# Weight write-back on GpSimd's queue, evacuations first on ScalarE, and weight sums in three spaced parts, in a retention layer with two feed-forward layers

## The chip, the cores and the metric

One core of a Trainium2 chip runs the whole program. The metric is the device time of one execution in microseconds (us), the median of several runs.

The engines are TensorE (PE, matrix products; PEld is its weight load), VectorE (DVE), ScalarE (ACT), GpSimd (POOL) and SyncE (SP). Each works through its own list of instructions in order and waits at the first one whose inputs are not there. A DMA is an instruction on the list of the engine that issues it.

## The reference

```
for t in range(S):                                  # retention, B=2, H=8, S=768, D=64
    state = gamma * state + outer(k[t], v[t])
    y[t] = scale * q[t] @ state
x = y as (1536, 512)
h = x @ w_in1;  g = softplus(h);  x = g @ w_out1     # 512 -> 2048 -> 512
h = x @ w_in2;  g = h * sigmoid(h);  out = g @ w_out2
```

Everything is fp32. The weights reach the chip as 64-bit numbers and are converted there.

## The kernel before, in words

Each fp32 matrix is split into a high part (rounded to the format that TensorE multiplies at full speed) and a low remainder, and one product is three matmuls: low x high, high x low, high x high.

**First layer.** After the retention chunks, 48 steps run: each is one of 16 column blocks `fc` of the first layer for one of three blocks of 512 tokens. `step(i)` issues, in this order, `first(i)` (12 matmuls into a bank `h`, then two softplus passes `act1` on ACT) and `second(i - 2)` (12 matmuls into the accumulators acc0 to acc3). The subtraction `act2(i)` on DVE makes the low part of `g`, which `second(i)` needs two steps later. The last step of a run of 3 to 5 blocks evacuates: acc0 and acc1 are copied out and seeded again on ACT (L512, L516), acc2 and acc3 are added out on DVE (L518). Until acc0 is seeded, the next `second` can't start.

**Conversion jobs.** In the gaps of DVE and ACT runs the conversion of weights, listed by `_jobs`: 64 tiles (16 `fc`, two layers, w_in and w_out) and 8 "forms". A tile is one exponent pass on ACT (L363, `w_exponent`), five or six DVE operations (L370 or L375 and L376, then L384, L387, L390, L392) and one rounding pass on ACT (L405, `w_split`). Tiles are loaded by SP (L335, three buffers; L344, the `near` copy, two buffers; the next load of a buffer is issued when its tile has been read).

**Forms.** The second layer's first product is done in seven half-size products per pair of column blocks (P1 to P7, by sums of quarter blocks as in Strassen's scheme, Winograd's form), so the weights of each pair need four sums. `w_sums` (DVE, L413 to L419) adds the two tiles' parts from `st1` into `w32` and makes the sums; `w_sums_high` (ACT, L422) rounds them; `w_keep` (DVE, L425) makes the remainders and writes everything to DRAM (`d1`, 1.8 MB, L428). The converted w_out tiles go through `st2` and `w32` to DRAM as `d2` (0.5 MB each, L409). There is one `st1` and one `w32`: the next pair's w_in tiles (L392 into `st1`) wait for the landing of `d1`, and the next `w_sums` (L413 into `w32`) waits for the landing of the `d2` write from `w32`. All these writes are issued by SP, in one list with the loads.

**Second layer.** 16 pair steps (two token halves of 8 pairs). A pair step issues the seven products in the order P1, P6, P2, P7, P5, P4, P3, and between them units (three matmuls each, L637) of the pair before. Three PSUM banks rotate over two buffers: `bx`, then `by` as a copy of `bx` (ACT, L677), then `bz`. P6 can't start until the copy is there; the copy needs P1 and a free buffer, which is that of the pair before's `bz`, read last by DVE at L695. `silu(q, c)` is two ACT passes (L619, L620) and one DVE subtraction (L621). Four of them per pair make `g`. The conversion jobs that are left (15) run in `slot()` after P1, P6 and P5.

Of the kernel before, what the change touches and what calls it, by code (L numbers as in the profile page):

```python
# [71 lines left out]
LATE = (43, 44, 45, 46, 47)  # L72


def _jobs(steps):


    first, last = {}, {}
    for i, (_, _, fc, _, _) in enumerate(steps):
        for s in range(2):  # L80
            first.setdefault((fc, s), i + LAG * s)
            last[fc, s] = i + LAG * s
    jobs = [("tile", 0, *u) for u in ((0, 0, -2), (1, 0, -1), (2, 0, 0), (0, 1, 2), (1, 1, 3), (2, 1, 4))]
    jobs += [("tile", 0, *u) for u in ((3, 0, 5), (4, 0, 6), (3, 1, 7))]
    left = sorted(set(first) - {j[2:4] for j in jobs}, key=lambda u: (first[u], u))
    second = []
    for p in range(NPR):
        a, b = 2 * p, 2 * p + 1
        second += [("tile", 1, a, 0), ("tile", 1, b, 0), ("forms", 1, p, 0), ("tile", 1, a, 1), ("tile", 1, b, 1)]
    room = 0.0  # L90
    for at in range(8, len(steps)):
        room = min(room, 3.0) + STEP_ROOM - 0.75
        i = at - LAG
        if steps[i][4]:
            room -= 1.4
        ready = [u for u in left if last.get((u[0] - NSLOT, u[1]), -1) < at]
        n = 0
        if ready and (room >= TILE_COST or first[ready[0]] <= at + 4):
            u = ready[0]
            assert at < first[u] - (u[1] == 0), (u, at, first[u])  # L100
            left.remove(u)
            jobs.append(("tile", 0, *u, at))
            room -= TILE_COST
            n += 1
        urgent = left and first[left[0]] <= at + 5
        if at >= 10 and at not in LATE and not urgent:
            while n < 2 and room >= (cost := FORMS_COST if second[0][0] == "forms" else TILE_COST):
                if second[0][0] == "forms" and jobs[-1][1] == 1 and jobs[-1][4] == at:
                    break
                jobs.append((*second.pop(0), at))  # L110
                room -= cost
                n = 2 if jobs[-1][0] == "forms" else n + 1
    assert not left
    return jobs + [(*j, None) for j in second]
# [17 lines left out]
def retention_ffn2_kernel(  # L132
# [268 lines left out]
    def w_split(u):  # L401
        _, l, fc, s, _ = tiles[u]
        a = conv_t.pop(u)[0]
        hi, lo = w_home(u)
        nc.scalar.activation(out=hi, in_=a, func=AF.Copy)  # L405
        w_t[l, fc, s] = (hi, lo)
        if l == 1 and s == 1:
            o = fc % 2 * 1024
            nc.sync.dma_start(out=d2[fc // 2][:, o : o + 1024], in_=(st2, w32)[fc % 2])  # L409

    def w_sums():

# [11 lines left out]
    def w_keep(p):  # L424
        nc.vector.tensor_tensor(  # L425
            out=st1[:, 3072:4096].bitcast(F32R), in0=st1[:, 3072:4096], in1=st1[:, 1024:2048], op=ALU.subtract
        )
        nc.sync.dma_start(out=_rows(d1[p], 2), in_=_rows(st1, 2)[:, :, QF:2048])  # L428

    h_t, g_t, acc_t = {}, {}, {}  # L430
    part = rp.rearrange("p (m t) -> p m t", m=4)
# [231 lines left out]
    def pair_step(q, fill, work):  # L663
# [10 lines left out]
        for n, (name, _, _) in enumerate(PRODUCTS):  # L674
            if name == "P1":
                product(q, n, new("bx"), True)
                nc.scalar.activation(out=new("by"), in_=bank["bx"], func=AF.Copy)  # L677
            elif name == "P6":
                product(q, n, bank["by"], False)
                nc.scalar.activation(out=c["u2"], in_=bank["by"], func=AF.Copy)  # L680
# [9 lines left out]
            elif name == "P4":  # L690
                product(q, n, bank["by"], False)
                silu(q, (1, 0), bank["by"])
            else:
                product(q, n, bank["bz"], False)
                nc.vector.tensor_tensor(out=c["c12"], in0=bank["bz"], in1=c["u2"], op=ALU.add)  # L695
                q1_load(q + 2)
            for w in work.get(name, ()):
                w()
            if name == "P5":
                silu(q, (1, 1), c["c22"])  # L700
            elif name == "P3":
                silu(q, (0, 1), c["c12"])
            for _ in range(gaps[n]):
                fill.pop(0)()
        q2_load(q + 1)
# [18 lines left out]
    def job_end(j):  # L724
        if j[0] == "tile":
            w_split(order[j[:4]])
        else:
            w_sums_high()

    def job_last(j):  # L730
        if j[0] == "forms":
            w_keep(j[2])

    split_units = []

    def step(i, more=()):
        nonlocal split_units
        first(i)
        ended = split_units
        for j in ended:  # L740
            job_end(j)
        split_units = units.get(i, [])
        for j in split_units:
            job_start(j)
        second(i - LAG)
        for j in split_units:
            job_main(j)
        for j in ended:
            job_last(j)
        act2(i)  # L750
        for w in more:
            w()

# [5 lines left out]
    with tc.manual_schedule():  # L759
# [149 lines left out]

        def slot():  # L910

            ended = before.copy()
            for j in ended:
                job_end(j)
            before.clear()
            if pending:
                j = pending.pop(0)
                if j[0] == "tile" and order[j[:4]] not in conv_t:
# [2 lines left out]
                    job_start(pending[0])  # L921
                job_main(j)
                before.append(j)
            for j in ended:
                job_last(j)

        x1 = []
        for q in range(NQ):
# [13 lines left out]
                    work[name], x1[:k] = tuple(x1[:k]), []  # L942
            pair_step(q, fill, work)
            fill = units_of(q)
        for f in fill:
            f()

# [59 lines left out]
```

## Time and profile before

| | us |
|---|---|
| median of 3 runs (lowest, highest) | 582.14 (579.09, 585.39) |
| the profiled execution: its time | 582.73 |
| its span | 580.6 |
| PE busy | 562.8 (97%) |
| DVE busy | 353.7 (61%) |
| ACT busy | 267.3 (46%) |
| POOL busy, all of it in the first 60 us | 25.6 (4%) |

The span is what the profiler saw; the 2.1 us between it and the time lie around it. PE's busy time is the sum of stretches in which a matmul is under way, so a matmul that runs at half clock counts as busy too. What can be gained without changing the matmuls is PE's idle time and the time lost to a lower granted clock. In the row of the page with 40 slices that clock is full but for slice 16 (0.7) and slice 26 (0.9).

### The profile page before, as it was taken

What the parts mean: (1) busy time and instruction counts of PE and PEld (TensorE: products, weight loads), DVE (VectorE), ACT (ScalarE), POOL (GpSimd) and SP (SyncE); (2) the same over time, 40 slices, a digit from 0 to 9 for tenths busy, and PEclk for the clock granted to TensorE, in tenths of its full rate; (3) what the DMA queues carried; (4) which work ended last, traced back from release to release, by engine and by line L of the source; (5) the groups of instructions that cost most, each with busy time, mean ns of one, the idle gap of its engine ahead of it and who ended that gap; (6) DMA issues with size and microseconds to landing.
All of it is one profiled execution on the core that took longest, in us unless ns stands there. A gap on an engine that the chain in (4) does not pass through costs nothing.

```text
span 580.6 us, 8107 instructions
## 1 busy us (share of the span) xinstructions
PE 562.8 (97%) x3122; PEld 479.9 (83%) x3122; DVE 353.7 (61%) x621; ACT 267.3 (46%) x500; POOL 25.6 (4%) x24
## 2 busy tenths in 40 slices
PE   8999999999989989999999999899999999999997
PEld 5888888888868867888788878788989999999996
DVE  2988837797887868696973896776553322212122
ACT  2355534565563634645654553553453333332322
POOL 1554000000000000000000000000000000000000
PEclk9999999999999997999999999899999999999999
DMA  8993333685997678788675789876920534444522
GB/s 297 399 411 112 109 110 110 216 304 204 358 355 271 238 263 317 277 330 300 225 274 214 294 298 360 335 305 251 339 82 20 195 116 170 165 183 185 200 72 108
DMA packets 30149, 136.04 MB, mean 234 GB/s; under 512 B 3360, under 2 KB 3360, under 8 KB 26272
## 3 DMA queue, kind: packets, MB, share of 16 engines
q1 hardware_dynamic: 30112, 135.54, 63.5%
q8 instruction: 24, 0.39, 0.3%
q14 instruction: 13, 0.11, 0.1%
HBM read 109.32 MB, written 26.21 MB: 233 GB/s over the span
## 4 chain that ended last, share of the span: by engine, by line
PE 71%; DVE 13%; DMA 9%; ACT 4%; issue 1%; SPq 1%; POOL 0%; DVEq 0%; POOLq 0%
PE acc L637 19%; PE acc L495 17%; PE h L455 15%; PE by L605 8%; PE bx L605 5%; PE bz L605 5%; DMA d<-w 4%; DMA near<-in_wts 2%; DVE rc L387 2%; DMA d<-st 1%; DMA rp<-in_att 1%; PE sc L235 1%; PE py L253 1%; DVE rc L384 1%; DVE rc L390 1%
## 5 line engine op out<-in xcount | busy, mean ns | idle before, releaser
L495 PE MATMUL acc<-rg,rw 128*128 128x512 f32 x564 | 140.0, 396 | 5.0 <-ACT acc L516 4.4
L455 PE MATMUL h<-rx,rw 128*128 128x512 f32 (+1 forms) x588 | 139.9, 387 | 0.1
L495 PEld LDWEIGHTS acc<-rg,rw 128*128 128x128 f32 x564 | 106.8, 191 | 29.2 <-ACT acc L516 5.9
L455 PEld LDWEIGHTS h<-rx,rw 128*128 128x128 f32 x588 | 109.0, 189 | 23.0 <-DVE rx L298 0.3
L637 PE MATMUL acc<-rw,rg 128*128 128x512 f32 x477 | 125.4, 392 | 0.0
L637 PEld LDWEIGHTS acc<-rw,rg 128*128 128x128 f32 x477 | 88.7, 188 | 12.3
L621 DVE TENSOR_TENSOR rg<-re,rg 128x384 fp32r<-128x384 f32 x53 | 29.3, 557 | 71.1 <-ACT re L620 71.1
L474 ACT ACTIVATE rg<-h 128x512 fp32r<-128x512 f32 x47 | 28.0, 596 | 92.2 <-PE h L455 92.1
L619 ACT ACTIVATE rg<-rp 128x384 fp32r<-128x384 f32 x32 | 16.8, 525 | 63.7 <-DVE rp L695 32.3
L387 DVE SCALAR_TENSOR_TENSOR rc<-rc 128x512 uint32<-128x512 uint32 x64 | 44.3, 692 | 2.2
L363 ACT ACTIVATE rc<-rc 128x512 f32<-128x512 f32 x64 | 41.5, 665 | 5.7 <-DMA rc<-in_wts 5.4
L384 DVE TENSOR_SCALAR rc<-rc 128x512 uint32<-128x512 uint32 x64 | 27.0, 422 | 16.8 <-ACT rc L363 16.8
L481 DVE TENSOR_TENSOR rg<-re,rg 128x512 fp32r<-128x512 f32 x47 | 34.0, 724 | 3.8 <-ACT re L475 3.7
L605 PE MATMUL by<-rx,rw 128*128 128x384 f32 x144 | 30.4, 347 | 4.8 <-ACT by L677 4.8
L605 PEld LDWEIGHTS by<-rx,rw 128*128 128x128 f32 x144 | 26.2, 192 | 8.2 <-ACT by L677 6.5
L689 DVE TENSOR_TENSOR rp<-bz,rp 128x384 f32<-128x384 f32 x16 | 8.9, 557 | 38.8 <-PE bz L605 38.8
L605 PE MATMUL by<-f,rw 128*128 128x384 f32 x144 | 29.2, 337 | 0.0
L390 DVE TENSOR_SCALAR rc<-rc 128x512 uint32<-128x512 uint32 x64 | 27.3, 427 | 2.2
L475 ACT ACTIVATE re<-h 128x512 f32<-128x512 f32 x48 | 28.5, 593 | 0.0
L605 PEld LDWEIGHTS by<-f,rw 128*128 128x128 f32 x144 | 25.9, 188 | 2.0
L405 ACT ACTIVATE rw<-rc 128x512 fp32r<-128x512 f32 x32 | 20.2, 633 | 15.7 <-DVE rc L387 15.7
L637 PE MATMUL acc<-rw,rx 128*128 128x512 f32 x99 | 27.1, 399 | 0.0
(86 smaller groups left out, 636.2 us busy)
## 6 DMA issues: line engine op xcount, KB each, us to landing
rc<-in_wts SPq DMA_DIRECT2D x64, 512.0 KB, 4.9
rw<-d SPq DMA_DIRECT2D x14, 1792.0 KB, 7.8
near<-in_wts SPq DMA_DIRECT2D x41, 511.5 KB, 4.7
d<-st SPq DMA_DIRECT2D x8, 1792.0 KB, 6.9
rw<-d SPq DMA_DIRECT2D x14, 1024.0 KB, 9.2
rp<-in_att SPq DMA_DIRECT2D x8, 512.0 KB, 7.5
d<-st SPq DMA_DIRECT2D x8, 512.0 KB, 8.6
d<-w SPq DMA_DIRECT2D x8, 512.0 KB, 9.2
```

What stands on the lines that cost most here:

```text
L363: nc.scalar.activation(out=z, in_=raw_t[u][:, :, 1].bitcast(F32), func=AF.Copy, scale=2.0**-112)
L384: nc.vector.tensor_scalar(out=z, in0=z, scalar1=3, scalar2=4, op0=ALU.logical_shift_left, op1=ALU.bitwise_or)
L387: nc.vector.scalar_tensor_tensor(out=a, in0=raw[:, :, 1], scalar=0x80000000, in1=z, op0=ALU.bitwise_and, op1=ALU.bitwise_or)
L390: nc.vector.tensor_scalar(out=z, in0=a, scalar1=0xFF800000, scalar2=None, op0=ALU.bitwise_and)
L455: nc.tensor.matmul(ph[:, t], lhsT=w[:, s], rhs=x[:, kc, t], start=kc == o == j == 0, stop=kc == NPAIR - 1 and j == 2, skip_group_check=i == 0,
L474: nc.scalar.activation(out=ghi, in_=ph, func=AF.Softplus)
L475: nc.scalar.activation(out=t, in_=ph, func=AF.Softplus)
L481: nc.vector.tensor_tensor(out=glo, in0=t, in1=ghi.bitcast(F32), op=ALU.subtract)
L495: nc.tensor.matmul(acc_t[m], lhsT=lhsT, rhs=rhs, start=first and j == 0 and not seeded, stop=last and j == 2, skip_group_check=m in SEEDED,)
L605: nc.tensor.matmul(to, lhsT=a[:, s], rhs=x[:, kc, :], start=start and kc == j == 0, stop=kc == 1 and j == 2, skip_group_check=True,)
L621: nc.vector.tensor_tensor(out=glo, in0=r, in1=ghi.bitcast(F32), op=ALU.subtract)
L637: nc.tensor.matmul(acc2_t[m], lhsT=a[:, s], rhs=b, start=start and j == 0, stop=stop and j == 2)
```

## The change

Five edits:

1. The writes of `d1` and `d2` are issued from GpSimd's list instead of SP's.
2. In a step that evacuates, the exponent passes (`job_start`) are issued behind `second` and its evacuation, not ahead of it.
3. The forms are spread out: `w_sums` in step i, `w_sums_high` at the end of step i + 1 (behind everything else that ACT does there), `w_keep` in step i + 2 behind the evacuation. Before, `w_sums_high` stood in step i + 1 ahead of the evacuation and `w_keep` at the end of the job work of step i + 1. In the second layer the slots are spread in the same way.
4. `not_before` keeps uses of `st1` and `w32` apart: a pair's first tile goes no earlier than three steps behind the forms before it, forms no earlier than two steps behind the last tile in `w32`. Of the list of jobs this moves two: tile (1, 4, 0) from step 27 to 28, where (1, 5, 0) already was, and tile (1, 8, 0) from step 39 to 40, where (1, 9, 0) already was.
5. In a pair step `silu` of P3's result goes behind the next pair's copy (L677 before), and `silu` of P5's result behind that of P4's.

```diff
+def not_before(job, done):
+    what, _, k, s = job
+    if what == "forms":
+        return max(done["tile", 1, 2 * k + 1, 0] + 1, done.get(("tile", 1, 2 * k - 1, 1), -9) + 2)
+    if s == 0:
+        return done.get(("forms", 1, k // 2 - 1, 0), -9) + 3
+    return max(done["forms", 1, k // 2, 0] + 1, done.get(("tile", 1, k - 2, 1), -9) + 2)
...
-                if second[0][0] == "forms" and jobs[-1][1] == 1 and jobs[-1][4] == at:
+                if at < not_before(second[0], done):
                     break
+                done[second[0]] = at
...
-            nc.sync.dma_start(out=d2[fc // 2][:, o : o + 1024], in_=(st2, w32)[fc % 2])
+            nc.gpsimd.dma_start(out=d2[fc // 2][:, o : o + 1024], in_=(st2, w32)[fc % 2])
...
-        nc.sync.dma_start(out=_rows(d1[p], 2), in_=_rows(st1, 2)[:, :, QF:2048])
+        nc.gpsimd.dma_start(out=_rows(d1[p], 2), in_=_rows(st1, 2)[:, :, QF:2048])
...
                 nc.scalar.activation(out=new("by"), in_=bank["bx"], func=AF.Copy)
+                if q:
+                    silu(q - 1, (0, 1), c["c12"])
...
                 silu(q, (1, 0), bank["by"])
+                silu(q, (1, 1), c["c22"])
...
-            if name == "P5":
-                silu(q, (1, 1), c["c22"])
-            elif name == "P3":
-                silu(q, (0, 1), c["c12"])
...
+    def job_after(j):
+        for p in to_split:
+            w_sums_high()
+            to_keep.append(p)
+        to_split.clear()
+        if j and j[0] == "forms":
+            to_split.append(j[2])
+
+    def job_keep():
+        for p in to_keep:
+            w_keep(p)
+        to_keep.clear()
...
         first(i)
-        ended = split_units
-        for j in ended:
+        for j in split_units:
             job_end(j)
         split_units = units.get(i, [])
-        for j in split_units:
-            job_start(j)
+        evacuates = steps[i - LAG][4]
+        if not evacuates:
+            for j in split_units:
+                job_start(j)
         second(i - LAG)
+        if evacuates:
+            for j in split_units:
+                job_start(j)
+        job_keep()
         for j in split_units:
             job_main(j)
-        for j in ended:
-            job_last(j)
         act2(i)
+        job_after(split_units[-1] if split_units else None)
...
-            ended = before.copy()
-            for j in ended:
+            for j in before:
                 job_end(j)
             before.clear()
+            job_keep()
+            done = None
...
-            for j in ended:
-                job_last(j)
+                done = j
+            job_after(done)
```

Line numbers of the changed kernel are higher by 12 to 15 (L422 is L434 there, L512 is L524, L677 is L689). First, ScalarE's list in steps 29 and 30, where the forms of pair 2 meet an evacuation; `st_883` is `st1`, `acc_0` and `acc_1` are the accumulators. Before:

```order
L474 ACTIVATE rg<-h_1868 128x512
L475 ACTIVATE re<-h_1868 128x512
L422 ACTIVATE st_883<-st_883 128x1024
L363 ACTIVATE rc<-rc 128x512 x2
L512 ACTIVATE rp<-acc_0_1724 128x512
L516 ACTIVATE acc_0_1893<-rp 128x512
L512 ACTIVATE rp<-acc_1_1727 128x512
L516 ACTIVATE acc_1_1896<-rp 128x512
```

And after the change:

```order
L486 ACTIVATE rg<-h_1868 128x512
L487 ACTIVATE re<-h_1868 128x512
L524 ACTIVATE rp<-acc_0_1722 128x512
L528 ACTIVATE acc_0_1890<-rp 128x512
L524 ACTIVATE rp<-acc_1_1725 128x512
L528 ACTIVATE acc_1_1893<-rp 128x512
L375 ACTIVATE rc<-rc 128x512 x2
L434 ACTIVATE st_883<-st_883 128x1024
```

The four evacuation passes have moved ahead of the rounding of the sums and of both exponent passes.

Second, ScalarE's list where the second layer's pair 2 ends (`by_2850` is its P4 bank) and pair 3 begins. Before:

```order
L619 ACTIVATE rg<-rp 128x384
L620 ACTIVATE re<-rp 128x384
L619 ACTIVATE rg<-by_2850 128x384
L620 ACTIVATE re<-by_2850 128x384
L619 ACTIVATE rg<-rp 128x384
L620 ACTIVATE re<-rp 128x384
L677 ACTIVATE by_2975<-bx_2968 128x384
L422 ACTIVATE st_883<-st_883 128x1024
L363 ACTIVATE rc<-rc 128x512
```

And after the change:

```order
L631 ACTIVATE rg<-by_2847 128x384
L632 ACTIVATE re<-by_2847 128x384
L631 ACTIVATE rg<-rp 128x384
L632 ACTIVATE re<-rp 128x384
L689 ACTIVATE by_2972<-bx_2965 128x384
L631 ACTIVATE rg<-rp 128x384
L632 ACTIVATE re<-rp 128x384
L375 ACTIVATE rc<-rc 128x512
L434 ACTIVATE st_883<-st_883 128x1024
```

The copy into `by` has moved ahead of the two passes of `silu` on P3's result.

Third, VectorE's list in steps 39 and 40, from the last operation of tile (1, 7, 1) on (`w_884` is `w32`). Before:

```order
L392 SCALAR_TENSOR_TENSOR w_884<-rc 128x512
L425 TENSOR_TENSOR st_883<-st_883 128x1024
L481 TENSOR_TENSOR rg<-re,rg 128x512
L518 TENSOR_TENSOR rp<-acc_2_2107,rp 128x512
L518 TENSOR_TENSOR rp<-acc_3_2111,rp 128x512
L370 TENSOR_SCALAR rc<-near 128x512
L384 TENSOR_SCALAR rc<-rc 128x512
L387 SCALAR_TENSOR_TENSOR rc<-rc 128x512
L390 TENSOR_SCALAR rc<-rc 128x512
L392 SCALAR_TENSOR_TENSOR st_883<-rc 128x512
L481 TENSOR_TENSOR rg<-re,rg 128x512
```

And after the change:

```order
L404 SCALAR_TENSOR_TENSOR w_884<-rc 128x512
L493 TENSOR_TENSOR rg<-re,rg 128x512
L530 TENSOR_TENSOR rp<-acc_2_2107,rp 128x512
L530 TENSOR_TENSOR rp<-acc_3_2111,rp 128x512
L437 TENSOR_TENSOR st_883<-st_883 128x1024
L493 TENSOR_TENSOR rg<-re,rg 128x512
L382 TENSOR_SCALAR rc<-near 128x512
L396 TENSOR_SCALAR rc<-rc 128x512
L399 SCALAR_TENSOR_TENSOR rc<-rc 128x512
L402 TENSOR_SCALAR rc<-rc 128x512
L404 SCALAR_TENSOR_TENSOR st_883<-rc 128x512
```

The remainders (L425, now L437), whose result the 1.8 MB write waits for, have moved behind the evacuation, and between them and the next tile into `st1` there is one subtraction of `act2` where two additions and one subtraction were; the next `act2` now follows two tiles.

## Rows read from the trace of the kernel before

**Rows 1.** Waits of PE from 60 us on: total us, times, longest.

```profile
PE by L605 <- ACT by L677: 4.8, 4, 3.0
PE acc L495 <- ACT acc L516: 4.4, 3, 3.1
PE acc L495 <- DVE rg L481: 0.6, 2, 0.4
PE bz L605 <- ACT re L620: 0.6, 1, 0.6
```

**Rows 2.** Busy time and granted clock (PEclk) of two stretches behind long waits.

```profile
219.00:224.00 5.00, 5.00 (x12) 3.89 (x13) 4.83 (x9) 3.67 (x7) 0.00 (x0) 0.50 0.87 296
364.00:367.00 3.00, 2.09 (x7) 2.09 (x8) 2.42 (x5) 2.42 (x5) 0.00 (x0) 0.68 0.97 410
```

**Rows 3.** The chain that ended last, in order of time: start us, us, what.

```profile
146.49 7.60 DMA near<-in_wts
...
202.10 10.53 DMA d<-w
...
218.94 5.49 PE acc L495 x12
224.43 3.15 PE h L455 x12
227.57 2.72 PE acc L495 x12
...
269.08 6.66 DMA d<-st
...
346.50 12.67 DMA d<-w
...
364.91 2.18 PE by L605 x6
367.09 2.08 PE acc L637 x6
370.23 1.39 PE acc L637 x6
...
379.95 1.06 PE bx L605 x6
```

**Rows 4.** ACT's instructions in order of time, at two long waits of PE.

```profile
215.60 1.06 ACT L422 ACTIVATE st<-st 128x1024 fp32r<-128x1024 f32 x1 [4.08 <-DVE st L419]
216.56 1.21 ACT L363 ACTIVATE rc<-rc 128x512 f32<-128x512 f32 x2
...
363.55 0.52 ACT L619 ACTIVATE rg<-rp 128x384 fp32r<-128x384 f32 x1 [5.59 <-DVE rp L695]
...
364.39 0.47 ACT L677 ACTIVATE by<-bx 128x384 f32<-128x384 f32 x1
```

**Rows 5.** DMA issues of the page: KB each, median us from issue to landing.

```profile
near<-in_wts SPq DMA_DIRECT2D x41, 511.5 KB, 4.7
d<-st SPq DMA_DIRECT2D x8, 1792.0 KB, 6.9
```

**Rows 6.** DVE's instructions in order of time, around two writes from `st1`.

```profile
194.76 1.22 DVE L425 TENSOR_TENSOR st<-st 128x1024 fp32r<-128x1024 f32 x1
...
267.84 1.22 DVE L425 TENSOR_TENSOR st<-st 128x1024 fp32r<-128x1024 f32 x1
...
275.83 0.69 DVE L392 SCALAR_TENSOR_TENSOR st<-rc 128x512 fp32r<-128x512 int32 x1 [3.12 <-DMA d<-st]
...
277.04 0.42 DVE L370 TENSOR_SCALAR rc<-near 128x512 uint32<-128x512 uint32 x1
...
279.64 0.68 DVE L481 TENSOR_TENSOR rg<-re,rg 128x512 fp32r<-128x512 f32 x1
```

**Rows 7.** PE's matmuls of `second` in steps 30 and 42.

```profile
210.24 2.88 PE L495 MATMUL acc<-rg,rw 128*128 128x512 f32 x12
...
282.53 2.88 PE L495 MATMUL acc<-rg,rw 128*128 128x512 f32 x12
```

More of the change, by code (lines that the diff above doesn't have):

```diff
@@ L89, in _jobs @@
         second += [("tile", 1, a, 0), ("tile", 1, b, 0), ("forms", 1, p, 0), ("tile", 1, a, 1), ("tile", 1, b, 1)]
+    done = {}
     room = 0.0
@@ L726, in job_end @@
             w_split(order[j[:4]])
-        else:
+    to_split, to_keep = [], []
+    def job_after(j):
+        for p in to_split:
             w_sums_high()
-    def job_last(j):
-        if j[0] == "forms":
-            w_keep(j[2])
+            to_keep.append(p)
[6 more added lines that the diff above has]
+        to_keep.clear()
     split_units = []
@@ L944, in retention_ffn2_kernel @@
             fill = units_of(q)
+        silu(NQ - 1, (0, 1), c_home["c12"])
         for f in fill:
```

## The prediction

> **What bounds the kernel now.** I read the table of waits first. PE is busy for 97% of the span, so the change can earn only what PE loses. From 60 us on PE waits in four groups [rows 1]: 4.8 us for the copy into `by`, 4.4 for the seeding of the accumulators, 0.6 for `act2`, 0.6 for the bank of P5; together 10.4 us. The reader is to see that they are few: ten waits, and two of them, 3.1 and 3.0 us, are over half of the sum.
>
> The second view is the clock. Behind the 3.1 us wait the granted clock is 0.50, the 1.2 GHz level, and behind the 3.0 us wait it is 0.68 on average [rows 2]. The chain prices that [rows 3]: 12 matmuls took 5.49 and the next 12 took 3.15 us, where 2.72 is usual, so 5.49 + 3.15 - 2 x 2.72 = 3.2 us. In the second layer it is (2.18 - 1.06) + (2.08 - 1.39) = 1.8 us. So PE loses 10.4 + 5.0 = 15.4 us in all, and no order of the other engines earns more.
>
> The third view is the chain, for the causes. Both long waits go back to a `d2` write of only 0.5 MB that took 10.53 and 12.67 us [rows 3], while a `d1` write of 1.8 MB takes 6.9 in the median [rows 5]. The small write stood in SP's queue behind larger transfers. In the first case `w_sums` waited for it, ACT waited 4.08 us for the sums, and the evacuation stood behind L422 and two exponent passes [rows 4]. In the second case DVE stood at L413, so L695 came late by 5.59 us for ACT; two passes of `silu` ran first, and then the copy [rows 4]. The seeding's other 4.4 - 3.1 = 1.3 us follow a stretch in which DVE was starved: a `near` load took 7.60 us behind 2.3 MB of writes, against 4.7 in the median [rows 3, 5].
>
> **The change part by part.** The profiled execution took 582.7 us, 0.6 above the median; I count from it.
>
> *Evacuations first on ACT (edits 2 and 3).* At the 3.1 us wait, L422 and the two exponent passes took 217.8 - 215.6 = 2.2 us, and ACT had waited 4.08 for the sums before that [rows 4]. In the changed order the four evacuation passes have no job in front of them that waits. They need only PE's own accumulators, so the 3.1 us and the 3.2 us of clock behind it go: 6.3 us. What is late instead are exponent passes, by the four passes of evacuation; DVE is itself behind its part of the evacuation then, so I take 0 for this, with 0.6 us of DVE as the upper bound.
>
> *Copies first (edit 5).* Copy and `silu` both wait for L695, so the copy comes earlier by exactly the two passes ahead of it, 364.39 - 363.55 = 0.84 us [rows 4]. That hides the three short waits for copies wholly, 4.8 - 3.0 = 1.8 us, and 0.8 of the 3.0. The postponed `silu` feeds units that stand two products further back, so it costs nothing. The 0.6 us at the bank of P5 has an exponent pass ahead of L422 now, which takes 0.6 out of the way: gone.
>
> *The writes on GpSimd's queue (edit 1).* GpSimd has nothing to do after 60 us, so waiting there stops nobody, and loads on SP's list no longer stand behind a write. The `d2` write behind the 3.0 us wait was issued at 346.5 and landed 12.7 us later [rows 3]; a landing 4 us sooner would do, an estimate from the 5.59 us that ACT waited for what stood behind it [rows 4]. Without the larger loads ahead of it I expect that. Then the other 2.2 us and 1.8 us of clock go. The starved tiles get their loads earlier, which is worth the 1.3 us of seeding and 0.2 of the waits for `act2`; I leave 0.5 of that in place because the same bytes still cross.
>
> *The cost: `w_keep` later, one `st1`.* The `d1` write now starts later and shares the DMA engines with loads instead of holding them up, and the next tile into `st1` waits for it. The trace has no write from GpSimd. I bound its time from issue to landing by 6.7 us (a `d1` write with little ahead) and 12.7 us (the worst write in the chain) [rows 3]. I take 10, nearest to the 10.53 of the write that shared the stretch with loads, since a `d2` write is now ahead of it on its queue. It shows in three places.
>
> Step 30: `w_keep` ended at 194.76 + 1.22 = 196.0 [rows 6]; behind `act2` and a later exponent pass it ends at 197.2. Landing at 207.2. Then come L392 (0.7), a whole second tile (279.64 - 277.04 = 2.6) and `act2` (0.7) [rows 6], since tile (1, 4, 0) moved to the same step as (1, 5, 0) and `act2` follows both: 211.2. PE wants it with the second of its matmuls, at 210.24 + 0.23 = 210.5 [rows 7]. A new wait of 0.7 us; by the bounds 0 to 3.4.
>
> Step 42: `w_keep` ended at 269.06 [rows 6]. It is now behind `act2` and two additions (+1.9), but L422 no longer holds up the tiles before (-1.0): 270.0. Landing at 280.0, plus the same 4.0: 284.0. PE wants it at 282.53 - 0.4 + 0.2 = 282.3, the 0.4 being the wait for `act2` that falls away [rows 1, 7]. A new wait of 1.7 us; by the bounds 0 to 4.4. Before, this landing held DVE up for 3.12 us [rows 6] and cost PE 0.4.
>
> Pair 4 of the second layer: between `w_keep` and the next tile's L392 stand two conversions and some subtractions, about 7 us, an estimate from the 2.6 us of a tile. At 10 us DVE is 3 late; the copy's 0.8 and about 1.3 of DVE's slack before P5's result cover most: 0.9 us; by the bounds 0 to 3.6. The other writes have steps to spare.
>
> *Sum.* Removed: 6.3 (long wait and clock in the first layer) + 4.8 (in the second) + 1.8 + 0.6 + 1.3 + 0.6 = 15.4. Back: 0.7 + 1.7 + 0.9 + 0.5 = 3.8. 582.7 - 15.4 + 3.8 = **571 us**. Waits of 1.7 us add no clock loss: the other two seeding waits, 1.3 us together, stand in a stretch with the clock at full.
>
> **The rivals.**
>
> *The queue gives nothing.* All transfers share the same DMA engines, so the small writes could land as late as before, and only ACT's order counts. Then 2.2 + 1.8 us of the second layer's wait stay, and 0.7 of the starved tiles' 1.3 (one exponent pass, 0.6, is out of the way): 567.3 + 4.0 + 0.7 + 3.3 = 575 us. For it: 2.3 MB of writes take the same time whoever issues them. Against it: landings follow the order of issue on SP's list, and the 0.5 MB write took longer than the 1.8 MB one [rows 3, 5], which is a queue, not a rate. The Trainium skill, page "DMA: Bandwidth & Descriptors", section "Issuing engines are not separate DMA queues", sides with this rival: it says that issuing from several engines saves only the time to issue. The rows speak against it as far as waiting behind others goes; no run here shows yet which holds.
>
> *GpSimd's writes are slow (slower than before).* If a `d1` write takes 15 us, the three places wait 5.7, 6.7 and 5.9 us, each with the clock loss that such a wait had, 3.2 + 3.2 + 1.8: 567.3 + 0.5 + 18.3 + 8.2 = 594 us. It decides from a landing of about 12.3 us on: there the waits are 3.0, 4.0 and 3.2, and one or two of them lose the clock, which makes up the 15.4. At the upper bound of 12.7 the time is 587. For it: DVE is busy nearly all the time in these stretches, and a tile's simpler operations run in 0.42 us where L392 with the same shape takes 0.69 [rows 6], so three of five run in a faster mode. Against it: a write is only wanted about 7 to 8 us after it starts, and one DMA should need far fewer of GpSimd's cycles than that. The Trainium skill, page "SBUF — State Buffer", section "SBUF: two separate sides", gives this a mechanism: descriptors of a DMA from GpSimd are written by GpSimd itself, through ports that VectorE locks in its faster mode, so the transfer starves. By that rule writes start late wherever tiles are converted; no run here shows it yet.
>
> *Given back in the middle.* Landings of 11.5 to 12 us, or one wait of 3 us more with its clock loss: 578 to 583, no change.
>
> **How the numbers follow.** Forecast (567 to 575): 0.60. Queue gives nothing (575): 0.13. Given back (578 to 583): 0.13. Slow writes (over 584): 0.14. The low end is 582.7 - 15.4 = 567.3, and 566.5 with the scatter of runs; little lies under it. The high end must take in the middle case: 582. The runs before spread from 579 to 585, so 1% is about what a measurement can tell. Faster by over 1% is under 576.3: most of the first two cases, 0.69. Slower by over 1% is over 588: 0.13. The rest, 0.18.
>
> **What would show it.** The waits for the seeding and for the copy should be gone, and the granted clock full from 60 us on. `act2` in steps 30 and 42 should be what PE waits for, 0 to 3 us each. `near` loads should stay near 5 us beside a write, `d2` writes come under 7, and `d1` writes lie between 8 and 11. I am wrong if `d1` writes take over 12 us, or if DVE's own operations get longer when GpSimd issues.

## The result, and the profile after

The changed kernel took 586.98 us in the median of 16 runs (582.46 to 616.99), the kernel before 583.85 us in 16 runs beside them. The ratio is 1.0062, with a 95% interval from 1.0032 to 1.0091: slower by about 0.6%, within the 1% that the prediction called no change, and far from the 571 us that it forecast. The ratio leaves out disturbed runs, such as the one of 616.99 us. The profiled execution has a span of 583.5 us, against 580.6 before.

First the waits of PE from 60 us on (total us, times, longest), the answer to [rows 1]:

```profile
PE acc L507 <- DVE rg L493: 7.8, 3, 3.3
PE by L617 <- ACT by L689: 3.5, 2, 3.3
PE bz L617 <- ACT re L632: 0.8, 1, 0.8
```

The seeding (L516 before) is gone from the list, and so are the short waits for copies but one of 0.2. In their place stand three waits for `act2`, where 0.6 us were, and one long wait for a copy, now in pair 4 and not in pair 3. The wait at the bank of P5, forecast to go, is 0.8 us where it was 0.6. PE waits 12.1 us where it waited 10.4. Here they are among PE's matmuls in order of time (start, us, the idle time before in brackets), the answer to [rows 7]:

```profile
168.76 4.38 PE L507 MATMUL acc<-rg,rw 128*128 128x512 f32 x11 [2.72 <-DVE rg L493]
...
216.03 4.39 PE L507 MATMUL acc<-rg,rw 128*128 128x512 f32 x11 [1.85 <-DVE rg L493]
...
286.51 2.79 PE L507 MATMUL acc<-rg,rw 128*128 128x512 f32 x11 [3.27 <-DVE rg L493]
...
384.27 2.29 PE L617 MATMUL by<-rx,rw 128*128 128x384 f32 x6 [3.34 <-ACT by L689]
```

These are step 22, step 30, step 42 and pair 4. Eleven matmuls take 2.79 us at the full clock, so behind the first two waits 4.38 us mean that the clock fell again. The windows say the same (columns as in [rows 2], the granted clock third from the right):

```profile
216.00:221.00 5.00, 4.97 (x15) 3.92 (x16) 4.46 (x8) 4.73 (x8) 0.00 (x0) 0.66 0.31 102
384.00:387.00 3.00, 2.73 (x8) 2.63 (x9) 1.87 (x4) 1.98 (x5) 0.00 (x0) 0.50 0.98 414
286.00:289.00 3.00, 2.49 (x11) 2.08 (x12) 2.93 (x6) 2.27 (x5) 0.00 (x0) 1.00 0.58 225
```

Waits of 1.85 and 3.34 us were followed by the 1.2 GHz level, one of 3.27 us was not.

The page's DMA issues answer to [rows 5] (KB each, median us from issue to landing):

```profile
near<-in_wts SPq DMA_DIRECT2D x41, 511.5 KB, 4.6
...
d<-st POOLq DMA_DIRECT2D x8, 1792.0 KB, 10.3
...
d<-st POOLq DMA_DIRECT2D x8, 512.0 KB, 4.7
d<-w POOLq DMA_DIRECT2D x8, 512.0 KB, 8.8
```

The `d1` write takes 10.3 us where it took 6.9. The `d2` writes, forecast to come under 7 us, take 4.7 from `st2` and 8.8 from `w32`. The page's section on queues, which had one queue for data before, has a second one for the writes (packets, MB, share of 16 engines):

```profile
q0 software_dynamic: 4480, 23.07, 9.9%
```

What the late `d1` write does is plainest in VectorE's list at step 42, the answer to [rows 6]:

```profile
270.47 1.22 DVE L437 TENSOR_TENSOR st<-st 128x1024 fp32r<-128x1024 f32 x1
271.60 0.69 DVE L493 TENSOR_TENSOR rg<-re,rg 128x512 fp32r<-128x512 f32 x1
...
282.45 0.69 DVE L404 SCALAR_TENSOR_TENSOR st<-rc 128x512 fp32r<-128x512 int32 x1 [7.00 <-DMA d<-st]
283.18 0.43 DVE L382 TENSOR_SCALAR rc<-near 128x512 uint32<-128x512 uint32 x1
...
285.16 0.69 DVE L404 SCALAR_TENSOR_TENSOR st<-rc 128x512 fp32r<-128x512 int32 x1
285.77 0.68 DVE L493 TENSOR_TENSOR rg<-re,rg 128x512 fp32r<-128x512 f32 x1
```

VectorE stands for 7.00 us at the first tile into `st1`, then does a second tile, and only then the `act2` that PE wants. The chain of pair 4 shows the other path, through L710 to the copy, the answer to [rows 3] and [rows 4]:

```profile
369.63 1.22 DVE st L437
...
371.14 10.32 DMA d<-st
381.56 0.69 DVE st L404
382.25 0.47 DVE rg L633
382.71 0.47 DVE rx L633
```

```profile
383.75 0.47 ACT L689 ACTIVATE by<-bx 128x384 f32<-128x384 f32 x1 [5.95 <-DVE rp L710]
```

In step 22 no `d1` landing is waited for: VectorE waited 2.26 and 2.65 us for two `near` loads that crossed with the `d1` write of 148.95 us, the second of them also with the `d2` write of 154.48 us. The rows below are VectorE's before the `act2` that step 22 wants.

```profile
160.03 0.43 DVE L382 TENSOR_SCALAR rc<-near 128x512 uint32<-128x512 uint32 x1 [2.26 <-DMA near<-in_wts]
...
165.42 0.43 DVE L382 TENSOR_SCALAR rc<-near 128x512 uint32<-128x512 uint32 x1 [2.65 <-DMA near<-in_wts]
...
168.02 0.69 DVE L493 TENSOR_TENSOR rg<-re,rg 128x512 fp32r<-128x512 f32 x1
```

**The balance.** Both kernels issue the same 3122 matmuls in the same order, so the start of each in one trace can be set against its start in the other. The difference grows or shrinks only at waits and at stretches of low clock (a wait here is how much later the next matmul starts, so it can differ a little from the idle time above):

| place | us, changed kernel against before |
|---|---|
| start-up, before 40 us | +1.4 |
| step 22: wait +2.5, clock +1.6 | +4.1 |
| step 30: wait +2.0, clock +1.7 | +3.7 |
| step 42: wait | +3.6 |
| pair 4: wait +3.5, clock +1.5 | +5.0 |
| bank of P5 | +0.2 |
| seeding waits gone: 1.9, and 6.3 with clock | -8.2 |
| waits for copies gone: 0.8, 0.2, 4.6 with clock, 0.9 | -6.5 |
| other `act2` waits gone | -0.7 |
| sum | +2.6 |

About 15 us went, as forecast; 16.6 came back where 3.8 were forecast. The start-up stands before any write of `d1` or `d2` and any pair step. The version with the copies alone had it too (1.1 us), and others that have all of the changed order did not, so it seems to belong to the execution and not to the change.

### The profile page after: what moved, and what is told of

Same layout as the page of the kernel before. It is cut to its first block, busy times and chain, and to the rows that moved or that the text cites. A ratio compares the mean times of both kernels' runs of the same rounds, so it can differ in the third digit from the quotient of the medians.

```text
span 583.5 us, 8130 instructions
## 1 busy us (share of the span) xinstructions
PE 560.9 (96%) x3122; PEld 479.9 (82%) x3122; DVE 354.4 (61%) x621; ACT 265.7 (46%) x500; POOL 40.1 (7%) x48
## 5 line engine op out<-in xcount | busy, mean ns | idle before, releaser
L649 PEld LDWEIGHTS acc<-rw,rg 128*128 128x128 f32 x477 | 89.0, 189 | 12.8
L396 DVE TENSOR_SCALAR rc<-rc 128x512 uint32<-128x512 uint32 x64 | 27.1, 424 | 15.5 <-ACT rc L375 15.4
L631 ACT ACTIVATE rg<-by 128x384 fp32r<-128x384 f32 x16 | 7.9, 492 | 48.8 <-PE by L617 48.8
L417 ACT ACTIVATE rw<-rc 128x512 fp32r<-128x512 f32 x32 | 20.2, 632 | 15.4 <-DVE rc L399 15.4
L404 DVE SCALAR_TENSOR_TENSOR st<-rc 128x512 fp32r<-128x512 int32 x24 | 16.6, 693 | 16.6 <-DMA d<-st 15.8
## 6 DMA issues: line engine op xcount, KB each, us to landing
d<-st POOLq DMA_DIRECT2D x8, 1792.0 KB, 10.3
```

The lines of the kernel that those rows point to most:

```text
L396: nc.vector.tensor_scalar(out=z, in0=z, scalar1=3, scalar2=4, op0=ALU.logical_shift_left, op1=ALU.bitwise_or)
L649: nc.tensor.matmul(acc2_t[m], lhsT=a[:, s], rhs=b, start=start and j == 0, stop=stop and j == 2)
```

## The experiments

**Theory A**: the `d1` write has a queue of its own, so loads that would have stood behind it on SP's list now run beside it and take their share of the same DMA engines; it lands late, and VectorE with it. **Theory B**: the later remainders (L437) and two tiles ahead of `act2` are enough, whichever engine issues. **Theory C**: a write issued by GpSimd is slow in itself. The waits below are those of one profiled execution of each version, which can lie some 3 us from the median of its runs.

**Both writes back on SP's list**, all else as changed:

```diff
-            nc.gpsimd.dma_start(out=d2[fc // 2][:, o : o + 1024], in_=(st2, w32)[fc % 2])
+            nc.sync.dma_start(out=d2[fc // 2][:, o : o + 1024], in_=(st2, w32)[fc % 2])
...
-        nc.gpsimd.dma_start(out=_rows(d1[p], 2), in_=_rows(st1, 2)[:, :, QF:2048])
+        nc.sync.dma_start(out=_rows(d1[p], 2), in_=_rows(st1, 2)[:, :, QF:2048])
```

> The changed kernel with all d1 and d2 writes back on SP's list (edit 1 undone), edits 2 to 5 kept. Theory A (the d1 write lands late because loads on another queue share the DMA engines with it): d1 lands 6 to 8.5 us after its issue instead of 10.3, PE's waits for act2 in steps 22, 30 and 42 (2.7, 1.85, 3.3 us) fall under 1.5 us each, the wait for the copy in pair 4 goes or shrinks, a wait for a late d2 write may come back; 577 to 582 us. Theory B (it is w_keep one step later and the two tiles in one step, whichever queue): the act2 waits stay over 1.5 us each; 584 to 588 us.

577.99 us, ratio 0.9937 (0.9895 to 0.9980). The `d1` issues of the page and PE's waits:

```profile
d<-st SPq DMA_DIRECT2D x8, 1792.0 KB, 7.9
```

```profile
PE acc L507 <- DVE rg L493: 5.1, 2, 3.0
PE by L617 <- ACT by L689: 2.0, 2, 1.8
PE bz L617 <- ACT re L632: 0.8, 1, 0.8
```

The waits of step 30 and pair 4 are gone, those of steps 22 (2.0) and 42 (3.0) are not, and one of 1.8 us has come for the copy of pair 3, behind a `d2` write of 11.5 us. Theory A can be seen in single loads. In the changed kernel the `near` load issued at 149.00 us, 0.05 us behind a `d1` write, landed after 4.1 us, ahead of the write (9.8 us). Here the `near` load issued at 148.18 us, 0.7 us behind the same write and in its list, landed after 7.8 us, behind it (7.2 us). So the queue is worth 1.25% (0.9937 against 1.0062), some 7 us, and something else keeps two waits alive.

**The kernel before with its writes on GpSimd's list** (edit 1 alone, the reverse of the diff above):

> The kernel before with edit 1 alone: d1 and d2 writes on GpSimd's list, the order of everything else as before. Theory A: d1 lands about 10 us after its issue instead of 6.9, so DVE waits longer for st1 and the evacuations behind it on ACT too; the 3.0 us copy wait goes, the seeding waits grow by 2 to 4 us; 582 to 588 us. Theory B: the queue alone is a gain, since the two long waits go back to d2 writes behind other transfers; 576 to 579 us.

580.93 us, ratio 0.9972 (0.9938 to 1.0007): no worse, perhaps a little better, and between what the two theories expected (582 to 588, 576 to 579). `d1` took 8.7 us. The 3.0 us copy wait of pair 3 was gone, as A forecast, with one of 1.9 in pair 4; the seeding waits, which A expected to grow, fell from 4.4 to 1.9, and `act2` waited 3.8. So the queue is not bad by itself; that the remainders, one step earlier, leave room for a later landing is the likely reason.

**The copies alone** (edit 5 in the kernel before):

```diff
                 nc.scalar.activation(out=new("by"), in_=bank["bx"], func=AF.Copy)
+                if q:
+                    silu(q - 1, (0, 1), c["c12"])
...
                 silu(q, (1, 0), bank["by"])
+                silu(q, (1, 1), c["c22"])
...
-            if name == "P5":
-                silu(q, (1, 1), c["c22"])
-            elif name == "P3":
-                silu(q, (0, 1), c["c12"])
...
+        silu(NQ - 1, (0, 1), c_home["c12"])
```

> The kernel before with edit 5 alone (silu of P3's result behind the next copy, silu of P5's behind that of P4's). Both theories: three short waits for copies (1.8 us together) go and the 3.0 us one becomes 2.2; 2 to 3 us less than before, 580 to 581 us where before has 583. If the copies wait for the bank and not for ACT, nothing changes.

582.5 us, ratio 0.9981 (0.9955 to 1.0007): not the 2 to 3 us less that were expected. The three short waits for copies went, the long one fell from 3.0 to 2.6, and 1.1 us of start-up, 1.3 more of `act2` and 0.8 more at the bank of P5 took most of it back in the profiled execution. A gain below what the runs can tell.

**`act2` first** in the changed kernel, ahead of the remainders and of the job's VectorE work:

```diff
+        act2(i)
         job_keep()
         for j in split_units:
             job_main(j)
-        act2(i)
```

> The changed kernel with one more move: in each step act2 is issued on DVE ahead of w_keep and of the job work, so that it no longer stands behind a tile that waits for a d1 write. Theory A: PE's waits for act2 (7.8 us and about 3 us of clock) go; up to 3 us come back as a seeding wait in step 22, whose evacuation stands behind late roundings on ACT; 576 to 580 us. If the late d1 landing reaches PE by another way (accumulators that DVE evacuates late, seeds): 583 us or more.

579.06 us, ratio 0.9922 (0.9890 to 0.9954), with `d1` still at 9.9 us. No wait for `act2` is left, a seeding wait has come:

```profile
PE acc L507 <- ACT acc L528: 3.7, 1, 3.7
PE by L617 <- ACT by L689: 2.3, 2, 2.1
PE bz L617 <- ACT re L632: 0.8, 1, 0.8
```

In step 22 the tiles are late (their loads are), and now the rounding pass of a late tile stands ahead of the evacuation on ScalarE. Theory B holds for the place of `act2`: it does not have to stand behind the tiles.

**Only the `d1` writes on SP's list** (the second pair of lines of the first diff):

> The changed kernel with one line undone: the 1.8 MB writes of d1 are issued from SP's list again, the d2 writes stay on GpSimd's. Theory A (the d1 write shares the DMA engines with the loads that stood behind it on SP's list, lands at 10.3 us instead of 6.9, and VectorE with act2 comes late): d1 lands at 8 us or under in the median, the wait of step 30 (1.9 us) and that of the copy in pair 4 (3.3 us) are gone or under 2, the time is 575 to 580 us, like the version with both writes on SP (578.0) or better by up to 3 us, since no d2 write stands ahead of a d1 write in step 42. Theory B (the later remainders and two tiles ahead of act2 alone, whatever the queue): steps 22, 30 and 42 still wait, 584 to 588 us.

578.64 us, ratio 0.9924 (0.9892 to 0.9956), `d1` 8.1 us. Step 30 kept 0.99, step 42 2.69, pair 4 1.52 us. As theory A expected.

**Only the `d2` writes on SP's list** (the first pair of lines):

> The changed kernel with the other line undone: the 0.5 MB writes of d2 on SP's list, the d1 writes on GpSimd's. Theory A: d1 still lands at about 10 us, the waits of steps 22, 30, 42 and pair 4 stay within 1 us of the changed kernel's 2.7, 1.9, 3.3 and 3.3, the time is 584 to 588 us. If instead it is the d2 write ahead of d1 on GpSimd's queue that makes d1 late: d1 lands under 8.5 us and the time is 576 to 580.

584.06 us, ratio 1.0029 (0.9996 to 1.0061), `d1` 9.6 us, waits of 3.26, 2.32, 2.00 for `act2`, 2.6 for the copy of pair 3 and 0.7 for that of pair 4:

```profile
d<-st POOLq DMA_DIRECT2D x8, 1792.0 KB, 9.6
```

So it is the 1.8 MB write, and not the small ones ahead of it, that makes the difference: on SP's list 0.992 to 0.994, on GpSimd's 1.003 to 1.006, wherever `d2` is. What moving `d2` does is to move the copy's wait: with `d2` on SP's list pair 3 waits 1.8 and 2.6 us and pair 4 0 and 0.7, with `d2` on GpSimd's pair 3 waits 0 and pair 4 1.5 and 3.3 (the first of each two with `d1` on SP's list). In the time it is not seen.

**Queues exchanged**: both writes on SP's list, and the loads of the weight tiles from step 10 on GpSimd's. No write is issued by GpSimd here.

```diff
-        nc.sync.dma_start(out=t, in_=wts[l, fc, s].bitcast(U32))
+        (nc.gpsimd if u >= NEAR[0] + 2 else nc.sync).dma_start(out=t, in_=wts[l, fc, s].bitcast(U32))
...
-        nc.sync.dma_start(out=t.bitcast(U16)[:, :n], in_=wts[l, fc, s].bitcast(U16)[:, 1 : 1 + n])
+        nc.gpsimd.dma_start(out=t.bitcast(U16)[:, :n], in_=wts[l, fc, s].bitcast(U16)[:, 1 : 1 + n])
```

> The changed kernel with its queues exchanged: from step 10 on the loads of the weight tiles (both copies) are issued from GpSimd's list, the writes of d1 and d2 from SP's. The d1 write is then on SP's list as in the kernel before, but apart from the loads. Theory A (it is the sharing with loads that makes the d1 write late, whoever issues it): d1 lands at 9.5 us or more in the median, act2 in steps 22, 30 and 42 and the copy of pair 4 wait for 12 to 18 us in all, the time is 583 to 589 us. Theory C (a write issued by GpSimd is slow in itself): d1 lands at 8 us or under, as with the writes on SP (7.9), and only loads are longer: under 580 us, or waits of a new kind for loads.

586.31 us, ratio 1.0049 (1.0025 to 1.0074): a loss like that of the changed kernel. The page's DMA issues and PE's waits:

```profile
near<-in_wts POOLq DMA_DIRECT2D x41, 511.5 KB, 5.1
...
d<-st SPq DMA_DIRECT2D x8, 1792.0 KB, 9.8
```

```profile
PE by L617 <- ACT by L689: 6.5, 2, 5.2
PE acc L507 <- DVE rg L493: 5.1, 3, 3.1
PE bz L617 <- ACT re L632: 1.0, 1, 1.0
PE acc L507 <- ACT acc L528: 0.6, 2, 0.5
```

As to the landing this decides between A and C: a `d1` write issued by SP is late too (9.8 us) once the loads are in another list. As to the time it does not. PE waits 13.2 us in all, but at the places for which A expected 12 to 18 it waits only 6.4: 1.85, 0.16 and 3.09 for `act2` in steps 22, 30 and 42, and 1.27 for the copy of pair 4. The longest wait is the copy of pair 3, behind a `d2` write that took 14.8 us on SP's list and kept VectorE standing:

```profile
361.42 1.23 DVE L425 TENSOR_TENSOR w<-st 128x1024 f32<-128x1024 f32 x1 [7.00 <-DMA d<-w]
```

```profile
366.26 2.29 PE L617 MATMUL by<-rx,rw 128*128 128x384 f32 x6 [5.19 <-ACT by L689]
```

So the loss as a whole is not that of `d1` alone here.

**All in GpSimd's list**: the changed kernel with those two load lines.

> The changed kernel with the loads of the weight tiles, from step 10 on, on GpSimd's list as well, so that loads and writes stand in one list again, GpSimd's and not SP's. Theory A: the loads behind a d1 write wait as they did on SP's list, d1 lands at 7 to 8.5 us, the wait of step 30 and that of the copy in pair 4 are under 2 us, and the time is that of the version with all on SP, 576 to 580 us. Theory C: GpSimd's descriptors are slow, d1 lands at 10 us or more, the loads get longer too, 587 us or more.

583.79 us, ratio 1.0008 (0.9979 to 1.0037). Half of it came as A expected: loads of the weight tiles and writes are in one list again (the reads of `d1` and `d2`, L600 and L604, stay on SP's), and `d1` lands after 8.3 us although GpSimd issues it; step 30 waits 1.28. The time did not, and lies between A's 576 to 580 and C's 587: 1.0 us came at the start-up, pair 3 waits 1.49 for its copy, and pair 4 still waits 3.26. In pair 4 GpSimd's own rows (start, us) show that the write was issued late:

```profile
369.09 0.53 POOL L347 DMA_DIRECT2D rc<-in_wts  x1 [12.70 <-DVE rc L402]
372.75 0.55 POOL L421 DMA_DIRECT2D d<-st  x1 [3.14 <-DVE rc L396]
373.29 0.70 POOL L440 DMA_DIRECT2D d<-st  x1
```

The remainders were done at 370.87, and the `d2` write ahead on the list had its data at 369.2, yet it went out at 372.75. What held GpSimd there stays open.

**Evacuations and copies first, nothing else**: the kernel before with edit 5 and, in steps that evacuate, exponent passes and L422 behind the evacuation; the remainders at their old place, list of jobs and SP's list as before.

```diff
+        evacuates = steps[i - LAG][4]
         for j in ended:
-            job_end(j)
+            if j[0] == "tile" or not evacuates:
+                job_end(j)
...
-        for j in split_units:
-            job_start(j)
+        if not evacuates:
+            for j in split_units:
+                job_start(j)
         second(i - LAG)
+        if evacuates:
+            for j in split_units:
+                job_start(j)
+            for j in ended:
+                if j[0] == "forms":
+                    job_end(j)
```

> The kernel before with the parts of the change that reorder ScalarE alone: exponent passes and the rounding of the sums behind the evacuation in steps that evacuate, and the copies ahead of silu. Remainders, list of jobs and SP's list as before. If the later remainders are what costs (theory B): the long seeding wait goes (3.1 us and 3.2 us of clock), no act2 wait of over 1 us comes in its place, the three short waits for copies go; the 3.0 us copy wait behind the late d2 write stays at 2 to 3 with its clock: 574 to 578 us. If every order that moves the rounding of the sums behind the evacuation delays the d1 write enough to make act2 late in step 30 or 42: waits of 2 us or more there and 579 to 582.

580.26 us, ratio 0.9954 (0.9927 to 0.9981): between both expectations, for a reason that neither named. The seeding wait went, but `act2` of step 31 came 2.50 us late in its place, with a slow stretch behind it:

```profile
213.16 1.22 DVE L413 TENSOR_TENSOR w<-st 128x1024 f32<-128x1024 f32 x1 [2.80 <-DMA d<-w]
...
222.99 1.22 DVE L425 TENSOR_TENSOR st<-st 128x1024 fp32r<-128x1024 f32 x1
224.12 0.69 DVE L481 TENSOR_TENSOR rg<-re,rg 128x512 fp32r<-128x512 f32 x1
```

VectorE itself had stood 2.80 us for the late `d2` write, as it had in the kernel before (2.67). Taking ScalarE's part of a wait away leaves VectorE's.

**`act2` first, with both writes on SP's list**:

> The changed kernel with both writes on SP's list and act2 issued ahead of the remainders and of the job's VectorE operations. Theory B says that the two waits left on SP's list (steps 22 and 42, 2.0 and 3.0 us, with 4 us of clock behind them) come from act2 standing behind two tiles: they go, and 578.0 becomes 572 to 575. Against that: a tile's result comes later by one subtraction (0.7 us), so its rounding pass comes later on ScalarE, ahead of the evacuation: a seeding wait of 2 to 4 us in step 22, as with act2 first alone (3.65), would leave 575 to 577. Theory A's part is not touched: the copy of pair 4 waits 1.8 us or less.

577.96 us, ratio 0.9896 (0.9862 to 0.9930): above both expectations. One seeding wait of 4.45 us in step 22, with 1.5 us of clock behind it (its 12 matmuls took 4.38 us, 2.88 is usual [rows 7]), and 2.7 us for copies. Step 42 no longer waits. With `act2` ahead the queue counts for less: 0.9896 against 0.9922, with intervals that overlap.

**The best of these parts in one kernel**: `d1` on SP's list, `d2` on GpSimd's, `act2` first, and in evacuating steps from 19 on the rounding pass of the step's tiles behind the evacuation.

```diff
+        evacuates = steps[i - LAG][4]
+        late = [j for j in split_units if evacuates and i > 18]
         for j in split_units:
-            job_end(j)
+            if j not in late:
+                job_end(j)
...
         second(i - LAG)
+        for j in late:
+            job_end(j)
```

> What the experiments point to, in one kernel: the changed kernel with the d1 writes on SP's list and the d2 writes on GpSimd's, act2 ahead of the remainders and of the job's VectorE operations, and in steps that evacuate (from step 19 on) the rounding pass of the step's tiles behind the evacuation. Theory A with B's share: act2 waits nowhere over 0.5 us, the seeding wait of step 22 (4.5 us and 1.6 us of clock with act2 first and all on SP) goes, the copies wait 2 to 3 us in all: 567 to 571 us. If the rounding pass is wanted there as early as it stood: a new wait of act2 or of the seeding of 2 us or more, and 572 to 576 us.

572.53 us (572.01 to 573.75), ratio 0.9837 (0.9819 to 0.9854): faster than both kernels, 1.5 us above the upper end of what theory A expected. It lies in the range of the other expectation, without its sign, a new wait of 2 us or more. That `d2` on GpSimd's list has a part in the gain is not shown. The profile has a span of 570.5 us and a granted clock of 1.00 throughout. PE's waits from 60 us on:

```profile
PE by L617 <- ACT by L689: 1.9, 2, 1.7
PE acc L507 <- ACT acc L528: 1.7, 2, 1.5
PE bz L617 <- ACT re L632: 0.8, 1, 0.8
PE acc L507 <- DVE rp L530: 0.6, 1, 0.6
```

5.0 us and no clock loss, where the kernel before lost 15.4: the difference, 10.4, is about the difference of the spans (10.1).

**The same with the `d1` writes on GpSimd's list**:

> The best version with one line put back as the change had it: the d1 writes on GpSimd's list again. If the sharing makes d1 late wherever it stands (theory A), d1 lands at 9.5 us or more, and PE pays only where VectorE has no slack left: the copy of pair 4 waits 3 us or more instead of 1.7, with some clock behind it, the seeding or act2 of steps 22, 30 and 42 less than 2 us more in all: 574 to 578 us. If with act2 first nothing hangs on the write any more: 572 to 573 us, as with d1 on SP's list (572.5).

575.49 us, ratio 0.9876 (0.9832 to 0.9920), `d1` 10.0 us. The interval touches that of the version above, so the runs alone hardly tell them apart; the profile does. The copy of pair 4 waits again, with half clock behind it, and no other new wait is over 0.4 us:

```profile
374.93 2.29 PE L617 MATMUL by<-rx,rw 128*128 128x384 f32 x6 [4.23 <-ACT by L689]
```

This is what theory A expected: here a late write costs where VectorE has no slack, and only there.

## Why the prediction was wrong

**What the change removes: right.** 15.4 us of loss were to go, and about 15 went: the long seeding wait with its clock, the long copy wait with its clock, the short ones; only the bank of P5 stayed. That the order of ScalarE alone does the first part was wrong: in the version with evacuations first on SP's list, 2.5 us came back as `act2`. With both writes on SP's list and the rest of the change it did go; there the remainders stand behind `act2`, and VectorE stood 0.33 us for that `d2` write where it had stood 2.67. Which of the two it took stays open.

**The landing of `d1`: right in size, wrong in what it touches.** 10 us were taken, 10.3 measured. Of the two reasons given, a stretch shared with loads and a `d2` write ahead on the same queue, only the first is needed: with `d2` on SP's list it still took 9.6. The exchange of queues showed that, and the return of all to one list (8.3 us).

**The failed step: what the queue gives ("The starved tiles get their loads earlier").** The sum credited the queue with 5.0 us: 2.2 and 1.8 for the long copy wait, 1.3 and 0.2 for the starved tiles, less 0.5. With all else as changed, the queue cost some 7 us instead. For `d2` it gave what was asked in the landing, nearly (9.4 us for the write that pair 3 waits for, after 12.7), but the copy's wait then came in pair 4. For the loads it charged the sharing to the write alone, and sharing is paid on both sides: loads issued beside the `d1` write of step 18 and the `d2` write behind it took up to 10.4 us, not near 5, VectorE waited 4.9 us for two of them, and step 22, which was not among the three places, waited 2.72 us. Not all of that is the queue's. PE's rows of step 22, before and with both writes on SP's list:

```profile
164.88 2.81 PE L495 MATMUL acc<-rg,rw 128*128 128x512 f32 x11 [0.22 <-DVE rg L481]
```

```profile
167.22 4.38 PE L507 MATMUL acc<-rg,rw 128*128 128x512 f32 x11 [2.04 <-DVE rg L493]
```

The load for the last tile ahead of this `act2` landed 2.8 us before TensorE came to step 22 in the kernel before, 1.0 us before with both writes on SP's list, and 0.3 us before in the changed kernel. So of the 2.5 us of new wait, 1.8 came with the rest of the change and 0.7 with the queue. The rest of the change issues the `d1` write at 147.5 us where it was issued at 144.3; that this is what makes the load late is likely and not shown by itself. With `act2` first, 3.65 us of seeding stood in place of the wait.

**The failed term: "Waits of 1.7 us add no clock loss".** The argument was two seeding waits of 1.3 us in all. In step 30 a wait of 1.85 us was followed by 1.7 us of clock loss, in step 22 one of 2.72 by 1.6, in pair 4 one of 3.34 by 1.5. That is 4.8 us of the 12.8 by which the return exceeds its forecast; the wait of step 22 is 2.5, and longer waits at the three places are 5.8 (less the 0.5 that the forecast had left in place for the loads).

**The three places.** Step 30: forecast 0.7, measured 1.85; the remainders ended where they were expected to, the write was issued 0.3 us behind them and took 0.8 longer than assumed; inside the bounds of 0 to 3.4. Step 42: forecast 1.7, measured 3.27; the remainders ended at 271.7 and not 270.0 (0.3 of that is the lag of the whole kernel there), 10.4 us of write behind that; also inside its bounds. Pair 4: forecast 0.9, measured 3.34; the gap from the remainders to the next tile was 7 us as estimated, but VectorE stood 3.85 us at the tile and PE 3.34 at the copy, so 0.5 us was covered and not the 2.1 assumed. Each term leaned to the cheap side of its bounds, and all three erred the same way, each for another reason: the landing, the later remainders, the cover.

**The rivals.** What happened is "given back in the middle" in its kind, waits of 3 us more with their clock loss, at 0.13; its landings of 11.5 to 12 us were not needed, and its 578 to 583 us were passed. The time lies in the band given to slow writes, whose cause was not seen. "The queue gives nothing" came out for `d2`, whose move is not seen in the time, and not for `d1`, whose move costs. "GpSimd's writes are slow" is not what was seen: the shortest `d1` write of the changed kernel, with little beside it, took 6.3 us, as the shortest before did (6.2), and a write by SP with the loads elsewhere was as late as one by GpSimd. Neither of the two signs of being wrong came: the longest `d1` write took 11.7 us, and VectorE was busy for 354.4 us against 353.7. The Trainium skill, page "SBUF — State Buffer", section "SBUF: two separate sides", says that GpSimd's descriptors starve while VectorE holds their shared port; by that rule the exchange of queues would have helped the write, and it landed after 9.8 us. One issue 3.1 us late, in the kernel with all in GpSimd's list, is the only row that could be read so. On the other page of the Trainium skill that was cited, "DMA: Bandwidth & Descriptors", section "Issuing engines are not separate DMA queues", the runs agree that the transfers share the DMA engines whoever starts them; that a second issuer changes no more than the time to issue they do not bear out: the list that the `d1` writes stand in decided between 0.992 and 1.006 here.

**What stays open.** Why a wait of 3.27 us kept the clock where 1.85 lost it, what held GpSimd's issue back in the kernel with all in its list, and why the copy's wait moves between pairs 3 and 4 with the list of `d2`.

## What to carry to other kernels

A long write taken off the list that it shares with loads no longer holds them up, but it shares the DMA engines with them: leave the one that a single buffer hangs on ahead of the loads in their list (here `d1`), and expect nothing from moving a short one until a run shows it (here `d2` only moved a wait). Before a producer is moved a step later, lay out every instruction between its landing and what TensorE wants, and move the wanted one (`act2`) ahead of the waiting one; in the changed kernel that was worth about as much as the queue (0.9922 and 0.9937 from 1.0062). Count a new wait of about 2 us at up to twice its length, since the clock may fall behind it.

## What the runs showed of the hardware

- A 1.8 MB write took 6.9 to 8.3 us in the median when loads stood behind it in the same list, on SP's or on GpSimd's, and 9.6 to 10.3 us when the loads had another list, again on either; before, in the kernel with its remainders a step earlier, it took 8.7 on GpSimd's.
- The granted clock fell behind waits of TensorE of 1.85, 2.72 and 3.34 us and stayed full behind one of 3.27 us, all in one execution. With the queues exchanged it stayed full behind one of 1.85 us (eleven matmuls in 2.79 us).
- GpSimd was busy for 0.53 to 0.70 us with each DMA that it issued, as the rows above show.
